# A hand-written order of steps in an attention and two mixture layers, written anew, instruction by instruction on TensorE

## The chip, the cores and the metric

The kernel runs on one core of one Trainium2 chip. The metric is device microseconds (us) of one execution: the median of three runs. One further execution was taken by the hardware profiler; all rows below are from that one. Its engines are called PE (TensorE matmul; PEld is its weight load), DVE (VectorE), ACT (ScalarE), POOL (GpSimd) and SP (SyncE, which here only issues transfers).

## The reference

```python
def reference(q, k, v, ...):               # q, k, v: [4, 8, 576, 64]
    attn = softmax(rot(q) @ rot(k).T / 8) @ v       # 32 heads, rot = rotary embedding
    x = attn as rows [2304, 512]
    x = moe(x, modality_id, ...)    # expert = argmax(x @ w_gate + bias); w * relu(x @ w1[e]) @ w2[e]
    return moe2(x, w_skip, ...)     # rows with x @ w_skip > 0 go through a second such layer, others pass
```

Each mixture layer has 8 experts, w1 of 512x1024 and w2 of 1024x512 each. Every row goes to one expert.

## The kernel before

The heads go through the attention in 16 pairs (p = 0 to 15; of a pair, head a is the odd one, b the even one). The 576 rows of a head are four chunks of 128 and a rest of 64; the rests of both heads share a chunk 4. For precision each operand is split in a high and a low part (`_hi` on ACT, `_lo` on DVE).

The work is cut in named steps. A pair has: `load` (SP), `rope0/1` for q and k (POOL; DVE for p = 0), `qk_tr0/1/2` (PE transposes), `qk_hi`, `qk_lo`, `stackq`, `stackk`, `stack2` (SP transfers, L385, that put parts of q and k beside each other), `v_hi`, `v_lo` (POOL); then for each chunk c and head: `s_mm` (4 matmuls, scores, L413), `s_max` (DVE, L426), `s_exp` (ACT, L430, writes PP), `t_mm` (4 transposes of PP, L508), `t_hi` (ACT, L511), `t_lo` (DVE, L515), `pv` (4 matmuls into O, L542); for chunk 4 `s_mm4`, `s_max4`, `s_exp4`, `t_mm4` (L521), `t_hi4`, `t_lo4` (DVE, L531, two instructions), and `l_mm`, `l_hi`, `l_lo` for the keys of the rest; at last `o_ev` (ACT, L551), `o_mm` (PE, L559), `o_norm` (DVE) and `x_store` (SP). After each fourth pair a batch of 576 rows is routed (`route1` to `route4p`) and its rows are put on the experts' lists with five indirect transfers, `scat0` to `scat4` (POOL, L783; each waits for the one before to land). After pair 11's batch, `ahead1` counts the rows per expert, `ahead2` starts to load the first expert's w1 (SP) and its first list blocks (POOL, L923), and `ahead3` gathers the first rows (POOL, L927), of the first three batches only. After the last pair, `w_hi/lo`, `w2_hi/lo` split the weights, `x_mm0/1` (L1048) transpose the first rows, `m_mm0..3` multiply them with w1, and the loop over blocks of rows begins.

PSUM holds two buffers T (for `qk_tr`, `t_mm`, `t_mm4`, `o_mm`, `route3`), two buffers S of two banks (for `s_mm`, `s_mm4`, `l_mm`) and one O. A step that takes a T buffer waits until the `_lo` (or `o_norm`) of the step two before it on T has read it; S is freed by `s_exp` or `l_lo`.

Each engine executes its instructions in the order in which they are written. That order is a table by hand: each step has a place `POS[name]`, pair p's steps are shifted by 10 p, and all are sorted by place.

Of the kernel before, what the change touches and what calls it, by code (L numbers as in the profile page):

```python
# [36 lines left out]


POS = dict(
    load=-24.542, rope0=-19.7644, rope1=-17.051, v_hi=-8.9048, v_lo=-8.1692, qk_tr0=-13.6414, qk_tr1=-12.311,  # L40
    qk_tr2=-13.5745, qk_hi0=-12.805, qk_hi1=-11.7868, qk_hi2=-12.5767, qk_lo0=-12.3488, qk_lo1=-11.4628,
    qk_lo2=-12.3321, stackq=-11.0409, stackk=-10.1724, stack2=-8.1426, s_mm0a=-6.6353,
    s_max0a=-6.358, s_exp0a=-6.1451, s_mm1a=-5.4139, s_max1a=-5.0991, s_exp1a=-4.5002, s_mm2a=-6.8226,
    s_max2a=-6.3673, s_exp2a=-6.3262, s_mm3a=-4.5196, s_max3a=-4.2702, s_exp3a=-3.2169, s_mm0b=0.5061, s_max0b=0.7184,
    s_exp0b=1.6424, s_mm1b=1.0912, s_max1b=1.4769, s_exp1b=2.2051, s_mm2b=-0.25, s_max2b=0.2617, s_exp2b=0.6341,
    s_mm3b=-2.98, s_max3b=-2.1652, s_exp3b=-0.0102, s_mm4=-3.5823, s_max4=-3.3036, s_exp4=-0.574, l_mma=2.0668,
    l_hia=2.4944, l_loa=2.889, t_mm0a=1.9202, t_hi0a=2.0731, t_lo0a=2.5799, pv0a=3.236, t_mm1a=0.4116, t_hi1a=0.8456,
    t_lo1a=1.3123, pv1a=5.4593, t_mm2a=-1.3533, t_hi2a=-0.4966, t_lo2a=-0.0415, pv2a=3.5848, t_mm3a=-0.2061,
    t_hi3a=0.2252, t_lo3a=0.5436, pv3a=4.2623, pv4a=6.1582, o_eva=7.9328, o_mma=11.0069, o_norma=11.4159,
    l_mmb=2.3316, l_hib=2.7629, l_lob=2.8995, t_mm0b=2.7857, t_hi0b=2.9519, t_lo0b=3.5072, pv0b=8.1446, t_mm1b=7.7762,  # L50
    t_hi1b=9.0218, t_lo1b=9.371, pv1b=9.8111, t_mm2b=4.1992, t_hi2b=5.0136, t_lo2b=5.3907, pv2b=9.1878, t_mm3b=5.9504,
    t_hi3b=5.9975, t_lo3b=6.2737, pv3b=9.6255, pv4b=10.7088, o_evb=11.2681, o_mmb=12.0371, o_normb=12.7355,
    t_mm4=2.9167, t_hi4=2.9782, t_lo4=4.275, r_inv=9.6079, x_store=37.2032, route1=14.3588, route2=22.2105, route2a=21.7, route2b=21.71, route2c=24.2, route2d=24.21, route2e=23.6,
    route2p=25.1759, route3=27.67, route4=27.675, route4p=31.787, scat0=36.7927, scat1=38.8708, scat2=41.493,
    scat3=47.44, scat4=50.0962, ahead1=35.9285, ahead2=50.2465, ahead3=67.8964, load2=10.4862, w_hi0=32.9026,
    w_lo0=41.1441, w_hi1=21.9224, w_lo1=51.4559, w_hi2=47.019, w_lo2=58.0083, w_hi3=69.8951, w_lo3=83.5081,
    x_mm0=28.1772, x_hi0=32.8113, x_lo0=40.2138, x_mm1=44.3621, x_hi1=44.6491, x_lo1=48.9724, m_mm0=54.5051,
    m_hi0=59.1976, m_lo0=60.9832, m_mm1=64.3611, m_hi1=70.0127, m_lo1=86.842, m_mm2=89.4447, m_hi2=98.112,
    m_lo2=121.9228, m_mm3=123.548, m_hi3=141.0569, m_lo3=171.334, route1z=50.3744, route2z=56.2551, route2pz=64.2831,
    route3z=76.7452, route4z=84.8667, route4pz=87.6679, scat0z=91.2443, scat1z=103.827, scat2z=116.579,  # L60
    scat3z=130.8944, scat4z=164.6592, w2_hi0=82.0097, w2_lo0=132.8461, w2_hi1=33.5145, w2_lo1=59.2958, w2_hi2=61.893,
    w2_lo2=91.8739, w2_hi3=15.1559, w2_lo3=69.1493, w2_hi4=109.0836, w2_lo4=179.4963, w2_hi5=91.8978, w2_lo5=142.0314,
    w2_hi6=71.166, w2_lo6=107.7054, w2_hi7=80.8631, w2_lo7=146.4834, const1=-14.5415, const6=-4.5415, const2=-2.2104,
    const3=3.6425, const4=7.7896, const5=-6.3575, warm1=-12.3105, warm2=-6.6348, warm3=-6.8221, warm4=44.3626,
    switch=10.7093,
)


# [1434 lines left out]
```

## Time and profile before

| what | us |
|---|---|
| median of three runs | 791.44 (791.17 to 794.57) |
| the profiled execution | 795.92 |
| its span, first to last instruction | 794.3 |

The profiled execution is 4.48 us above the median; 1.6 us of it lie outside the span. PE is busy in 729.6 us of the span, DVE in 510.8, ACT in 434.8, POOL in 370.2. A busy time is a union of pipelined instructions: four scores that follow each other in 0.52 us are each shown with some 0.3 us.

### The profile page before, as it was taken

To read this page: it belongs to the slowest core of one execution; us is meant where nothing else is said; L and a number is where in the kernel's file an instruction comes from. 1 tells how busy PE (TensorE), PEld (TensorE's weight loads), DVE (VectorE), ACT (ScalarE), POOL (GpSimd) and SP (SyncE) were. 2 spreads that over 40 slices of the span, in tenths; PEclk is the share of its full clock that TensorE was granted. 3 is DMA by queue.
4 is the path that set the end of the run, shared out by engine and by line. 5 is a ranking of instruction groups with operands and counts; after the bars stand their busy time and mean duration, and the time that the engine had idled before them with its cause. 6 is when DMAs were issued, how large, how long until landed. Compare 5 with 4: busy or idle time off the path is not lost. (4 is left out here: it accounts for less than half of the span.)

```text
span 794.3 us, 15318 instructions
## 1 busy us (share of the span) xinstructions
PE 729.6 (92%) x4948; PEld 655.1 (82%) x4948; DVE 510.8 (64%) x1216; ACT 434.8 (55%) x940; POOL 370.2 (47%) x498
## 2 busy tenths in 40 slices
PE   7789999999999999985979999999999979999994
PEld 6688888888888889885878899889988968877773
DVE  5688888888888888873442323232535653588882
ACT  2677777777787787762312222222224542278781
POOL 6385556776676665205343233323434422134532
PEclk9899999999999999996989999999999989999998
DMA  5644445555454553482011111011395401578910
GB/s 136 156 102 117 108 123 129 129 121 124 115 131 121 129 126 80 91 241 69 1 41 35 48 41 54 16 53 41 95 322 173 170 18 38 208 254 293 327 54 18
DMA packets 75197, 92.27 MB, mean 116 GB/s; under 512 B 29440, under 2 KB 50176, under 8 KB 75090
## 3 DMA queue, kind: packets, MB, share of 16 engines
q1 hardware_dynamic: 65938, 73.74, 33.1%
q0 software_dynamic: 7200, 12.46, 5.1%
q10 hardware_dynamic: 1952, 4.85, 2.0%
q8 instruction: 42, 0.69, 0.4%
q14 instruction: 65, 0.53, 0.3%
HBM read 62.11 MB, written 12.95 MB: 95 GB/s over the span
## 5 line engine op out<-in xcount | busy, mean ns | idle before, releaser
L413 PE MATMUL S<-w1s 128*128 128x288 f32 x640 | 116.0, 308 | 3.7 <-ACT PP L430 2.8
L1118 PE MATMUL psY<-w2s,hT 128*128 128x512 f32 x480 | 119.3, 397 | 0.0
L1069 PE MATMUL psM<-xT,w1s 128*128 128x256 f32 x864 | 113.1, 288 | 0.0
L430 ACT ACTIVATE PP<-S,nm 128x576 f32<-128x576 f32 x128 | 95.3, 745 | 30.6 <-DVE nm L426 29.6
L1069 PEld LDWEIGHTS psM<-xT,w1s 128*128 128x128 f32 x864 | 107.4, 192 | 0.6 <-issue 0.6
L426 DVE TENSOR_REDUCE nm<-S 128x1 f32<-128x576 f32 x128 | 96.3, 753 | 8.4 <-PE S L413 7.8
L1118 PEld LDWEIGHTS psY<-w2s,hT 128*128 128x128 f32 x480 | 87.2, 188 | 16.8
L413 PEld LDWEIGHTS S<-w1s 128*128 128x128 f32 x640 | 91.7, 190 | 8.9 <-ACT PP L430 3.6
L515 DVE TENSOR_TENSOR tl<-T,th 128x512 fp32r<-128x512 f32 x128 | 88.0, 688 | 15.9 <-ACT th L511 14.9
L508 PE MATMUL T<-ident,PP 128*128 128x128 f32 x512 | 79.6, 279 | 7.0 <-DVE w1s L382 6.1
L511 ACT CAST th<-T 128x512 fp32r<-128x512 f32 x128 | 74.8, 584 | 19.1 <-PE T L508 18.3
L508 PEld LDWEIGHTS T<-ident,PP 128*128 128x128 f32 x512 | 61.1, 142 | 12.1 <-DVE w1s L382 9.3
L1082 DVE SCALAR_TENSOR_TENSOR hT<-psM,hT 128x512 fp32r<-128x512 f32 x36 | 24.9, 691 | 69.4 <-ACT hT L1077 57.5
L1342 PE MATMUL psM<-w1s,xT 128*128 128x512 f32 x240 | 63.5, 410 | 4.9 <-DVEq L1265 4.5
L1382 PE MATMUL psY<-w2s,hT 128*128 128x512 f32 x240 | 63.8, 403 | 4.4 <-DVE hT L1361 4.4
L1077 ACT ACTIVATE hT<-psM 128x512 fp32r<-128x512 f32 x36 | 21.5, 598 | 76.8 <-PE psM L1069 76.3
L313 POOL TENSOR_TENSOR mem_w<-qkn,mem_w 128x640 f32<-128x640 f32 x30 | 46.5, 1551 | 36.2 <-PE T L350 28.7
L937 POOL DMA_INDIRECT list<-tg,si x20 | 21.1, 1056 | 90.4 <-issue 57.3
L542 PE MATMUL O<-th,vh 128*128 128x288 f32 x256 | 60.2, 316 | 0.5 <-ACT os L551 0.5
L1342 PEld LDWEIGHTS psM<-w1s,xT 128*128 128x128 f32 x240 | 45.0, 193 | 16.3 <-ACTq L1265 4.6
L1382 PEld LDWEIGHTS psY<-w2s,hT 128*128 128x128 f32 x240 | 43.0, 188 | 15.4 <-DVE hT L1361 6.9
L542 PE MATMUL O<-tl,vh 128*128 128x288 f32 x256 | 54.6, 295 | 0.0
(263 smaller groups left out, 1407.2 us busy)
## 6 DMA issues: line engine op xcount, KB each, us to landing
raw<-in_moe_w_dram SPq DMA_DIRECT2D x20, 512.0 KB, 6.4
mem_w<-in_moe_w_dram SPq DMA_DIRECT2D x20, 512.0 KB, 5.7
w1s<-w1s SPq DMA_DIRECT2D x30, 256.0 KB
raw1b<-in_moe_w_dram SPq DMA_DIRECT2D x12, 512.0 KB, 5.8
raw2b<-in_moe_w_dram SPq DMA_DIRECT2D x12, 512.0 KB, 5.8
w1s<-w1s SPq DMA_DIRECT2D x16, 288.0 KB, 3.1
qkn<-in_q_dram SPq DMA_DIRECT2D x16, 256.0 KB, 3.5
qkn<-in_k_dram SPq DMA_DIRECT2D x16, 256.0 KB, 3.5
```

The source lines that it names most:

```text
L313: eng.tensor_tensor(r, x, tb[:, i, 0].unsqueeze(1).broadcast_to([128, 2, 5, D]), op=ALU.mult)
L413: nc.tensor.matmul(ps[:, hf, 0:288], s["wide"][:, o : o + 128], s["K"][h % 2][:, kk, hf * 288 : hf * 288 + 288], start=first and kk == 0, ...
L426: nc.vector.tensor_reduce(st[h // 2]["nm"][:, h % 2, c : c + 1], hs[h]["ps", c][:, :, 0:288], axis=AX.XY, op=ALU.max, negate=True)
L430: nc.scalar.activation(PP[:, c, h % 2 * S : h % 2 * S + S].rearrange("p (a b) -> p a b", a=2), hs[h]["ps", c][:, :, 0:288], AF.Exp, bias=s ...
L508: nc.tensor.transpose(ps[:, c * 128 : c * 128 + 128], PP[:, c, o : o + 128], ident)
L511: nc.scalar.copy(hs[h]["th"][:, j, 0:512], hs[h]["tp", j])
L515: nc.vector.tensor_tensor(s["tl"][:, j, 0:512], s["tp", j], s["th"][:, j, 0:512].bitcast(F32), op=ALU.subtract)
L542: nc.tensor.matmul(s["ot"][:, hf, 0:288], st[h // 2]["vh"][:, h % 2, j].rearrange("p s d -> p (s d)"), w[:, hf * 288 : hf * 288 + 288], st ...
L1069: self.nc.tensor.matmul(ps[:, a], self.w1s[:, wi, dc, fs], x[:, xi, dc], start=(dc == 0 and wi + xi == 0), stop=(dc == 3 and wi == 1))
L1118: nc.tensor.matmul(ps, h[:, hi, f, t * 128 : t * 128 + 128], w2s[:, wi, f], start=(f == 0 and hi + wi == 0), stop=(f == 7 and hi == 1))
L1342: nc.tensor.matmul(ms[hf], x[:, xi, dc], w1s[:, wi, dc, hf * 512 : hf * 512 + 512], start=(dc == 0 and wi + xi == 0), stop=(dc == 3 and xi ...
L1382: nc.tensor.matmul(y, hT[:, hi, f], w2s[:, wi, f], start=(f == 0 and hi + wi == 0), stop=(f == 7 and hi == 1))
```

## The change

Every number of `POS` is another one. A step of PE has now one place for each of its instructions, so that instructions of several steps can alternate. `x_mm` keeps its PSUM buffer by place, so that `x_mm1` may stand before `x_hi0`. No instruction is added or taken away.

For a middle pair p, from one `s_mm2a` to the next (steps of other pairs with their distance; `.0` to `.3` are instructions of a step):

- PE before: s_mm2a, pv0a-1, s_mm0a, pv2a-1, t_mm2b-1, pv3a-1, s_mm1a, pv1a-1, s_mm3a, t_mm3b-1, pv4a-1, qk_tr0+1, s_mm4, qk_tr2+1, s_mm3b, qk_tr1+1, t_mm1b-1, pv0b-1, t_mm2a, pv2b-1, pv3b-1, s_mm2b, t_mm3a, pv1b-1, t_mm1a, s_mm0b, pv4b-1, o_mma-1, s_mm1b, t_mm0a, o_mmb-1, l_mma, l_mmb, t_mm0b, t_mm4.
- PE after: s_mm2a, pv0a.2, pv2a.0, s_mm0a, pv0a.3, rest of pv2a, pv3a.0, t_mm2b, rest of pv3a, pv1a.0, s_mm1a, rest of pv1a, t_mm3b, qk_tr0.0-2, s_mm3a, qk_tr0.3, pv4a, qk_tr2, s_mm4, qk_tr1, t_mm1b, pv0b, half of pv2b, s_mm3b, t_mm2a, rest of pv2b, half of t_mm3a, s_mm2b, rest of t_mm3a, pv3b, pv1b.0, t_mm1a and s_mm0b in turns, pv1b, pv4b and o_mma in turns, s_mm1b, t_mm0a, o_mmb, l_mma, pv0a.0 (of p), l_mmb, t_mm0b, t_mm4, pv0a.1.
- ACT: `v_hi` of p stands ahead of `s_exp2a` (before: `v_hi` of p+1 behind `t_hi1a`), `t_hi2b` ahead of `s_exp0a`, `t_hi3b` ahead of `s_exp1a`; `qk_hi0`, `qk_hi2` and `o_eva` ahead of `s_exp3a`.
- DVE: `t_lo2b` stands ahead of `s_max1a`, `t_lo3b` ahead of `s_max3a`, `qk_lo0` and `qk_lo2` ahead of `s_max4`, `qk_lo1` and `t_lo1b` ahead of `s_max3b`.
- POOL: rope1+1, v_lo, rope0+2 (before: rope0+2, v_lo+1, rope1+2). `scat0` to `scat4` of a batch stand 20 to 26 earlier in the table's scale, of which 15 is the shift that the scores have too.
- SP: x_store-2, load+2, stackq+1, stackk+1, stack2+1 (before: load+2, x_store-4, then the same).
- Start: 68 of the 76 dummy transposes stand ahead of the first `qk_tr0` (before: 36), and `const5` (14 small DVE instructions) ahead of the first `rope0` (before: behind `s_max0a` of pair 0).
- End: `scat0` and `scat1` of pair 11's batch now stand before `s_mm2a` of pair 15, `scat4` between that pair's `s_mm3b` and `s_mm2b`, and the gather `ahead3` before its `s_mm1b`, where it was directly before `x_mm0`; `load2` (w2) follows `x_store` of pair 14. PE goes x_mm0, x_mm1, m_mm3, m_mm0, route3, m_mm1, m_mm2; DVE has six `w2_lo` between `x_lo1` and `m_lo3`, and then route2, route4, `w_lo2`.

```diff
-    load=-24.542, rope0=-19.7644, rope1=-17.051, v_hi=-8.9048, v_lo=-8.1692, qk_tr0=-13.6414, qk_tr1=-12.311,
...
-    s_max0a=-6.358, s_exp0a=-6.1451, s_mm1a=-5.4139, s_max1a=-5.0991, s_exp1a=-4.5002, s_mm2a=-6.8226,
...
+    load=-36.7017, rope0=-33.9451, rope1=-30.111, v_hi=-21.4821, v_lo=-18.1897,
+    qk_tr0=(-30.6061, -30.6042, -30.5936, -30.1223), qk_tr1=(-28.4904, -28.4904, -28.4848, -28.4848),
...
+    s_mm2a=(-22.2316, -22.2316, -22.2316, -22.2316), s_max2a=-21.7162, s_exp2a=-21.4126,
...
+    route2p=7.9451, route3=10.8285, route4=11.1643, route4p=13.5564, scat0=15.9086, scat1=17.0957, scat2=21.6619,
+    scat3=22.8497, scat4=24.3127, ahead1=20.7865, ahead2=24.8061, ahead3=26.173, load2=-9.6073, w_hi0=-4.399,
...
                 for hf in range(2):
-                    nc.tensor.matmul(
+                    yield nc.tensor.matmul(
                         ps[:, hf, 0:288],
...
         def s_mm(h, c):
             ps = hs.setdefault(h, {})["ps", c] = pp.tile([128, 2, 512], F32, name="S")
-            scores(ps, h, c * 128 + (S + 128) * (h % 2), True, True)
+            yield from scores(ps, h, c * 128 + (S + 128) * (h % 2), True, True)
...
         def at(base, name, f, *args):
-            steps.append((base + POS[name], len(steps), f, args))
+            where = POS[name]
+            if isinstance(where, tuple):
+
+                f, args = next, (f(*args), None)
+            else:
+                where = (where,)
+            for x in where:
+                steps.append((base + x, len(steps), f, args))
...
-        ps = self.x_ps = self.bank("T")
+        ps = self.bank("T")
+        self.x_ps = {**self.__dict__.get("x_ps", {}), o: ps}
```

## Rows read from the trace of the kernel before

**Rows 1.** Busy time by stretch: us, then PE, PEld, DVE, ACT, POOL (instructions), PEclk, DMA, GB/s

```profile
39.90:327.80 287.90, 271.33 (x2134) 253.47 (x2133) 246.82 (x490) 229.96 (x550) 186.26 (x227) 1.00 0.49 119
183.53:203.96 20.43, 19.34 (x155) 18.08 (x154) 17.50 (x35) 16.38 (x40) 12.97 (x12) 1.00 0.54 131
```

**Rows 2.** Timeline of PE, `t_mm4`: start us, us, of pair 0 and of pair 14

```profile
39.25 0.60 PE L521 MATMUL T<-ident,PP 128*128 128x128 f32 x4
...
327.18 0.60 PE L521 MATMUL T<-ident,PP 128*128 128x128 f32 x4
```

**Rows 3.** Timeline of PE in one pair; in brackets idle time and what ended it

```profile
208.25 0.43 PE L542 MATMUL O<-th,vh 128*128 128x288 f32 x2
...
208.78 0.68 PE L413 MATMUL S<-w1s 128*128 128x288 f32 x4
209.30 0.60 PE L508 MATMUL T<-ident,PP 128*128 128x128 f32 x4
209.66 0.51 PE L542 MATMUL O<-Y,vh 128*128 128x288 f32 x2
210.27 0.63 PE L347 MATMUL T<-ident,mem_w 128*128 128x128 f32 x4
...
212.15 0.79 PE L413 MATMUL S<-w1s 128*128 128x288 f32 x4
213.50 0.63 PE L347 MATMUL T<-ident,mem_w 128*128 128x128 f32 x4 [0.55 <-DVE w1s L382]
...
214.67 0.42 PE L542 MATMUL O<-tl,vh 128*128 128x288 f32 x2
215.53 0.66 PE L508 MATMUL T<-ident,PP 128*128 128x128 f32 x4 [0.43 <-DVE w1s L382]
```

**Rows 4.** Groups of instructions, whole span: count, busy us, mean ns, idle before

```profile
L430 ACT ACTIVATE PP<-S,nm 128x576 f32<-128x576 f32 x128 | 95.3, 745 | 30.6 <-DVE nm L426 29.6
...
L426 DVE TENSOR_REDUCE nm<-S 128x1 f32<-128x576 f32 x128 | 96.3, 753 | 8.4 <-PE S L413 7.8
...
L515 DVE TENSOR_TENSOR tl<-T,th 128x512 fp32r<-128x512 f32 x128 | 88.0, 688 | 15.9 <-ACT th L511 14.9
...
L511 ACT CAST th<-T 128x512 fp32r<-128x512 f32 x128 | 74.8, 584 | 19.1 <-PE T L508 18.3
```

**Rows 5.** Timeline of the other engines in the pair of Rows 3

```profile
207.22 1.39 DVE L531 TENSOR_TENSOR Y<-T,Y 64x512 fp32r<-64x512 f32 x2
...
211.55 1.04 ACT L370 CAST w1s<-T 128x512 fp32r<-128x512 f32 x3
...
212.50 9.45 SPq L385 DMA_DIRECT2D w1s<-w1s  x10
212.67 0.94 DVE L382 TENSOR_TENSOR w1s<-T,w1s 128x512 fp32r<-128x512 f32 x3
```

**Rows 6.** Dummy transposes (L583) by stretch: us, PE (x), PEld (x), PEclk, DMA, GB/s

```profile
1.70:7.50 5.80, 5.80 (x27) 5.80 (x28) 1.00 0.93 285
7.60:8.70 1.10, 1.08 (x10) 0.84 (x8) 1.00 0.77 193
...
14.40:17.70 3.30, 3.21 (x16) 3.30 (x17) 0.50 0.22 45
```

**Rows 7.** Timeline of the start: first instruction of `const5`, `s_mm4` of pair 0

```profile
21.54 0.43 DVE L193 CAST w<-w8i 128x8 f32<-128x8 int32 x1
...
26.26 1.33 PE L413 MATMUL S<-w1s 128*128 128x288 f32 x8 [2.49 <-ACT PP L430]
```

**Rows 8.** Timeline of the end of the attention and the first block

```profile
329.66 0.98 POOL L783 DMA_INDIRECT list<-g_tg,g_si  x1 [3.24 <-DMA list<-g_tg,g_si]
...
357.55 0.79 POOL L923 DMA_DIRECT2D list<-list  x1 [9.24 <-DMA list<-g_tg,g_si]
...
366.19 1.09 PE L1048 MATMUL T<-ident,xg 128*128 128x128 f32 x4 [10.10 <-DMA xg<-out_dram,tok]
...
402.10 0.17 PE L1168 MATMUL psG<-oh,U 128*128 128x8 bf16 x1 [4.64 <-DVE oh L1165]
```

More of the change, by code (lines that the diff above doesn't have):

```diff
@@ L39 @@
 POS = dict(
-    load=-24.542, rope0=-19.7644, rope1=-17.051, v_hi=-8.9048, v_lo=-8.1692, qk_tr0=-13.6414, qk_tr1=-12.311,
-    qk_tr2=-13.5745, qk_hi0=-12.805, qk_hi1=-11.7868, qk_hi2=-12.5767, qk_lo0=-12.3488, qk_lo1=-11.4628,
-    qk_lo2=-12.3321, stackq=-11.0409, stackk=-10.1724, stack2=-8.1426, s_mm0a=-6.6353,
-    s_max0a=-6.358, s_exp0a=-6.1451, s_mm1a=-5.4139, s_max1a=-5.0991, s_exp1a=-4.5002, s_mm2a=-6.8226,
-    s_max2a=-6.3673, s_exp2a=-6.3262, s_mm3a=-4.5196, s_max3a=-4.2702, s_exp3a=-3.2169, s_mm0b=0.5061, s_max0b=0.7184,
@@ L45 @@
[L45 to L63, printed above, removed]
@@ L64 @@
-    const3=3.6425, const4=7.7896, const5=-6.3575, warm1=-12.3105, warm2=-6.6348, warm3=-6.8221, warm4=44.3626,
-    switch=10.7093,
+    load=-36.7017, rope0=-33.9451, rope1=-30.111, v_hi=-21.4821, v_lo=-18.1897,
+    qk_tr0=(-30.6061, -30.6042, -30.5936, -30.1223), qk_tr1=(-28.4904, -28.4904, -28.4848, -28.4848),
+    qk_tr2=(-29.2463, -29.2463), qk_hi0=-29.4052, qk_hi1=-27.2491, qk_hi2=-29.202, qk_lo0=-29.1934, qk_lo1=-26.9027,
+    qk_lo2=-28.9941, stackq=-25.8754, stackk=-23.011, stack2=-22.5711,
@@ new lines @@
+    s_mm0a=(-22.0577, -22.0577, -22.0577, -22.0577), s_max0a=-21.4825, s_exp0a=-20.8972,
+    s_mm1a=(-21.3076, -21.3076, -21.3076, -21.3076), s_max1a=-20.1346, s_exp1a=-19.5976,
+    s_mm2a=(-22.2316, -22.2316, -22.2316, -22.2316), s_max2a=-21.7162, s_exp2a=-21.4126,
+    s_mm3a=(-20.5225, -20.5225, -20.5225, -20.5225), s_max3a=-19.2489, s_exp3a=-17.295,
+    s_mm0b=(-14.3536, -14.1043, -14.0042, -13.9921), s_max0b=-12.9587, s_exp0b=-12.9046,
+    s_mm1b=(-13.0069, -12.9105, -12.9105, -12.9105), s_max1b=-12.8704, s_exp1b=-12.8563,
@@ new lines @@
+    s_mm2b=(-15.4526, -15.4526, -15.4386, -15.4386), s_max2b=-14.6158, s_exp2b=-14.0784,
+    s_mm3b=(-16.5055, -16.5055, -16.5055, -16.5055), s_max3b=-15.336, s_exp3b=-15.2119,
+    s_mm4=(-19.1859, -19.1807, -19.1807, -19.1807, -19.1807, -19.1807, -19.1807, -19.1331), s_max4=-17.2632,
+    s_exp4=-16.1016, l_mma=(-12.7178, -12.6968, -12.6968, -12.6968, -12.6968), l_hia=-12.6823, l_loa=-12.3966,
+    t_mm0a=(-12.9092, -12.9092, -12.9092, -12.9092), t_hi0a=-12.8887, t_lo0a=-12.6464,
+    pv0a=(-12.6813, -12.3155, -12.1921, -12.051), t_mm1a=(-14.662, -14.3587, -14.3361, -14.0627), t_hi1a=-14.0257,
@@ new lines @@
+    t_lo1a=-12.9105, pv1a=(-11.482, -10.94, -10.9025, -10.9025), t_mm2a=(-16.3817, -16.3207, -16.3207, -16.3207),
+    t_hi2a=-15.4958, t_lo2a=-15.2606, pv2a=(-12.0718, -11.7295, -11.7295, -11.7295),
+    t_mm3a=(-16.0635, -15.4829, -15.3061, -15.3061), t_hi3a=-14.423, t_lo3a=-14.3448,
+    pv3a=(-11.6779, -11.4985, -11.4827, -11.4827), pv4a=(-10.0997, -9.6192), o_eva=-8.4242,
+    o_mma=(-3.8821, -3.1843, -3.04, -3.0069, -3.0069), o_norma=-2.9092,
+    l_mmb=(-12.5752, -12.5752, -12.5752, -12.5752, -12.5752), l_hib=-12.3276, l_lob=-12.2073,
@@ new lines @@
+    t_mm0b=(-12.4134, -12.3969, -12.3818, -12.3818), t_hi0b=-12.2316, t_lo0b=-11.9973,
+    pv0b=(-6.7017, -6.7017, -6.7017, -6.5129), t_mm1b=(-7.8953, -7.8953, -7.8953, -7.4024), t_hi1b=-6.7199,
+    t_lo1b=-6.1978, pv1b=(-5.2632, -4.5696, -3.9061, -3.5847), t_mm2b=(-11.6405, -11.6405, -11.6405, -11.6405),
+    t_hi2b=-11.3076, t_lo2b=-11.3076, pv2b=(-6.5077, -6.5077, -6.2903, -6.172),
+    t_mm3b=(-10.8705, -10.8705, -10.8705, -10.8705), t_hi3b=-9.8594, t_lo3b=-9.5279,
+    pv3b=(-5.2659, -5.2659, -5.2659, -5.2659), pv4b=(-3.1789, -3.0274), o_evb=-3.008,
@@ new lines @@
+    o_mmb=(-2.908, -2.9041, -2.9041, -2.8421, -2.8421), o_normb=-2.5794,
+    t_mm4=(-12.3715, -12.3715, -12.3715, -12.3715), t_hi4=-11.4863, t_lo4=-11.4473, r_inv=-4.0473, x_store=-1.9435,
+    route1=-0.138, route2=22.2105, route2a=0.0711, route2b=2.3991, route2c=5.809, route2d=6.9931, route2e=3.0369,
+    route2p=7.9451, route3=10.8285, route4=11.1643, route4p=13.5564, scat0=15.9086, scat1=17.0957, scat2=21.6619,
+    scat3=22.8497, scat4=24.3127, ahead1=20.7865, ahead2=24.8061, ahead3=26.173, load2=-9.6073, w_hi0=-4.399,
@@ new lines @@
+    w_lo0=-2.8576, w_hi1=-10.8843, w_lo1=-10.3037, w_hi2=-3.048, w_lo2=429.3001, w_hi3=-3.3916, w_lo3=-3.1985,
+    x_mm0=-2.5275, x_hi0=-2.4128, x_lo0=-2.2031, x_mm1=-2.35, x_hi1=-2.1246, x_lo1=-2.0387, m_mm0=48.2393,
+    m_hi0=181.3328, m_lo0=1552.441, m_mm1=611.0564, m_hi1=1628.6892, m_lo1=1629.4085, m_mm2=1553.3863, m_hi2=1625.391,
+    m_lo2=1629.4891, m_mm3=6.3202, m_hi3=25.9681, m_lo3=44.977, route1z=0.3768, route2z=49.5846, route2pz=83.0433,
+    route3z=164.2886, route4z=197.8744, route4pz=247.5439, scat0z=1554.3317, scat1z=1556.1501, scat2z=1556.8609,
@@ L66 @@
+    scat3z=1626.076, scat4z=1629.4488, w2_hi0=3.7676, w2_lo0=6.9592, w2_hi1=0.3352, w2_lo1=2.9321, w2_hi2=-0.7596,
+    w2_lo2=-0.5096, w2_hi3=-2.8008, w2_lo3=-0.4501, w2_hi4=4.8596, w2_lo4=46.894, w2_hi5=-2.8731, w2_lo5=-2.4756,
+    w2_hi6=5.4516, w2_lo6=35.4726, w2_hi7=-0.1195, w2_lo7=1.6545, const1=-11.4827, const6=-0.4859, const2=-2.0544,
+    const3=21.5765, const4=22.9241, const5=-41.9989, warm1=-42.8466, warm2=-28.4242, warm3=-36.7926, warm4=1629.4689,
+    switch=-2.9023,
 )
@@ L441, in s_mm4 @@
             for i in range(2):
-                scores(ps, 2 * p + i, 512 + 64 * i, i == 0, i == 1)
+                yield from scores(ps, 2 * p + i, 512 + 64 * i, i == 0, i == 1)
         def s_max4(p):
@@ L507, in t_mm @@
             for c in range(4):
-                nc.tensor.transpose(ps[:, c * 128 : c * 128 + 128], PP[:, c, o : o + 128], ident)
+                yield nc.tensor.transpose(ps[:, c * 128 : c * 128 + 128], PP[:, c, o : o + 128], ident)
         def t_hi(h, j):
```

24 lines of the change are left out of this document (12 added, 12 removed).

## The prediction

> **What bounds the kernel now.** I read four views. The busy time by stretch comes first [rows 1]: from 39.9 to 327.8 us PE is busy in 94% of the time, DVE in 86% and ACT in 80%. No engine is full, yet none has much room. The timeline of one step that occurs once in each pair [rows 2] gives the pace: from `t_mm4` of pair 0 to that of pair 14 it is (327.18 - 39.25) / 14 = 20.57 us for a pair. The timeline of PE inside a pair [rows 3] shows where PE's 20.4 us go. Scores, transposes and `pv` that follow each other without a wait start every 0.52, 0.36 and 0.53 us for four instructions (208.78 to 209.30, 209.30 to 209.66, 208.25 to 208.78). At three places the next start comes later than that: `qk_tr0` (210.27 - 209.66 - 0.26 = 0.35), `qk_tr1` (213.50 - 212.15 - 0.53 = 0.82) and `t_mm2a` (215.53 - 214.67 - 0.26 = 0.60), 1.77 us together. The last two name DVE L382, that is `qk_lo`: PE waits for a T buffer. The busy column hides this, since ends of matmuls overlap with waits. At last the end of the attention [rows 8]: PE has nothing from 356.1 (366.19 - 10.10) to 366.19, because the first rows come late, and they come late because the list block waited 9.24 us for a scatter to land.
>
> DVE can't be read as free: in the 20.43 us of the one pair shown it works 17.50 [rows 1]. A pair can't fall below that, whatever PE's order.
>
> **Instructions.** None is added. PE has 155 multiplications and 154 weight loads in a pair [rows 1], so each instruction loads its own weights already, and taking turns between steps costs no further load. I price the splitting at nothing; the bounds are the 0.08 us by which `pv` starts later than the pace at some changes of step, and as much gained.
>
> **The middle pairs.** I walked once around the new order with the old durations: a reduction 0.75 us, an exponential 0.74, a `t_hi` 0.58, a `t_lo` 0.69 [rows 4], `t_lo4` 1.39, three `qk_hi` 1.04, three `qk_lo` 0.94 [rows 5], and 0.1 us from a reader's end to the next writer of the buffer. Clock zero is the first `l_mma`.
>
> - `qk_tr1` takes the buffer of `qk_tr0`. Before, ACT did `s_exp3a` and DVE `s_max4` ahead of its readers. Now `qk_hi0` and `qk_lo0` come first; the buffer is free at 9.66, when PE has just ended `s_mm4` at 9.53. Wait 0.13 instead of 0.82.
> - `t_mm2a` takes that of `qk_tr1`. `qk_lo1` now precedes `s_max3b`, and PE has `t_mm1b`, `pv0b`, two `pv2b` and `s_mm3b` to do first (1.7 us of work where it had 0.9). Free at 11.82, PE there at 11.74. Wait 0.08 instead of 0.60.
> - `qk_tr0` takes that of `t_mm2b`, whose `t_lo2b` still stands behind the 1.39 us of `t_lo4`: free at 6.88, and PE is there at 6.53. Wait 0.35, as before. Behind it now stands `s_mm3a`, so `s_max3a` starts later too; DVE covers this with `s_max1a` and `t_lo3b` (until 8.07, and the scores are ready at 7.9).
> - `t_mm3b` now stands ahead of `s_mm3a` and waits for `t_lo4` itself: free at 6.18, PE there at 5.90. New wait 0.28.
> - `s_mm3b` needs the S buffer of `s_exp3a`, which ACT now does after `qk_hi` and `o_eva`: free at 10.57, PE comes at 11.21. Nothing.
> - The `pv0a.0` and `.1` fill time in which PE waited for `t_mm4` and `s_mm2a`: 0.25 gained.
>
> The balance is 0.69 + 0.52 + 0.25 - 0.28 = 1.18, plus some small waits that I don't count apart; I take 19.2 us for a pair. 14 pairs of 20.57 - 19.2 give **19.2 us**. Bounds: by the walk without any delay between engines 18.7 (26 us), and half of the balance (8 us).
>
> What else is queued: SP issues ten transfers for `stack` in 9.45 us from `qk_hi2` on [rows 5]. In the walk this begins at 9.2, and the first scores of the next pair come at 20.8, so 2 us remain. `load` waits on SP for `v_lo`, which now comes later (6.4 of the walk); the three transfers behind it end at 8.4, before the `stack` ones are due. POOL does its 12.97 us [rows 1] with one pair more of lead; a batch's `route1` between `rope0` and `rope1` can push `v_lo` and so SP by some 2 us, once in four pairs. It is covered by those 2 us; without cover it would cost 3 x 2 = 6 us. `x_store` two pairs earlier is three issues ahead of `load`; nothing reads the rows so soon.
>
> **The start.** 68 dummies now precede `qk_tr0`. Before, 27 took 5.80 us and the next 10 took 1.08 [rows 6], 0.215 and 0.108 us each. The PEclk column reads 1.00 in both stretches, but where it reads 0.50 the pace is 0.2 again, so the slow pace is that of the level of 1.2 GHz. The 68 take 5.8 + 41 x 0.108 = 10.2 us and end at 11.9, when `qk_tr0` once could begin after 36 (8.7). The Trainium skill, page "TensorE: Matmul & The Clock Gate", section "Part 4: PE-mode transpose", says that transposes don't make the full clock engage; rows 6 speak against it, since only transposes ran before the pace doubled. `const5` (14 instructions from 21.54 on; 3 us by my estimate, more than the wait that it caused) goes ahead of `rope0` on DVE, partly into its wait for the first load. Together I let the first scores start 1.5 us later, since `qk_tr2` needs the second `rope` anyway. Back come the 2.49 us that PE waited at 26.26 for the exponential behind `const5` [rows 7], and by my estimate 1 us of latencies after it. Net **-2 us**; bounds +3.4 (all dummies in the way, nothing back) and -5.
>
> **The end.** The idle 10.1 us go if the rows land when PE ends. From `t_mm4` of pair 14 PE needed 356.1 - 327.18 = 28.9 us to the end of the attention, now some 27.5. A scatter takes POOL 3.24 + 0.98 = 4.2 us with its wait for the one before [rows 8]. By its new place `scat0` is issued some 7 us ahead of that `t_mm4`, so `scat4` 17 us later, at +10. It lands 3.2 us after (as the others) or 9.2 (as this one did, with the weights' loads on the queues; w2 now waits for pair 14's `x_store`). From the list's load to `x_mm0` it took 366.19 - 357.55 = 8.6. So the rows land at +22 to +28 against PE's 27.5. I keep 1 us of wait. After that the pace is POOL's: in the row of 402.10 PE waits for a selection that hangs on POOL's work, 35.9 us after `x_mm0`. `route2` now stands on DVE behind six `w2_lo`; one us later. Net **-8 us**; bounds 0 (the gather is as late as before) and -12 (all the idle time and the 1.4 us that PE ends earlier).
>
> **Sum.** 795.92 - 19.2 - 2 - 8 = 766.7 for the profiled execution; the median is 4.48 lower: 762.2. I say **762**, its own range 749 to 772.
>
> **Rivals.**
>
> 1. The stall only moves. PE's order of steps is nearly the old one, DVE works 17.5 us in it, and a wait that is shorter for `qk_tr1` comes back at the next T buffer. For it: 0.28 at `t_mm3b` is such a return. Against it: four changes on DVE and ACT all put readers of T first. Only start and end and half a us per pair remain: 791.4 - 10 - 3 = 778 to 784. Chance 0.20.
> 2. A convoy at the T buffers, the slower side. `t_mm3b` and `qk_tr0` now stand on PE ahead of `s_mm3a`. PE is in order: if `t_lo4` slips (its `t_hi4` has `t_hi0b` ahead on ACT, and `v_hi` behind it delays `s_exp2a`), `s_mm3a` slips with it, DVE runs out of reductions, and the next `t_lo` is late again. One more reduction (0.75) waited for at each of `t_mm3b`, `qk_tr0` and `qk_tr2`, and 0.5 for `s_mm1a`, give 19.2 + 2.75 = 21.95 a pair, 14 x 1.38 = +19, less 10: 800. It decides from 21.3 a pair on (0.7 above today's, which uses up the 10). Chance 0.12.
> 3. The end gives nothing: scatters still behind w1's load, or w2, now loaded later, holds up ACT's `w2_hi5` in front of `x_hi0`. 770. Chance 0.10.
> 4. The dummies never reach the quick pace. 68 x 0.215 = 14.6 us, `qk_tr0` at 16.3 instead of 11.9: 766. Rows 6 speak against it; chance 0.02. This is what the Trainium skill's sentence above ("TensorE: Matmul & The Clock Gate", Part 4) would make of it.
> 5. All of it cancels, a pair at some 21.2: 788 to 795. Chance 0.06.
>
> The forecast has 0.50. From 748 (26 + 5 + 12 us gained) to 785 lie the forecast and rivals 1, 3 and 4, 0.82. Faster by over 0.5% (4 us, about what a measurement of this kernel can tell from no change): 0.82; within it 0.06; slower 0.12.
>
> **What would show it.** `t_mm4` of pairs 0 and 14 in the new profile some 269 us apart; no wait over 0.2 us before `qk_tr1` and `t_mm2a`, one of 0.3 before `t_mm3b`; `x_mm0` with an idle time of 0 to 2 us; the first dummies ending near 12 us. Wrong is the forecast if the pair stays above 20 us, where I would look at what DVE does while PE waits for T; or if PE idles before `x_mm0` as long as now.

## The result, and the profile after

The changed kernel takes 768.97 us (median of 4 runs, 767.88 to 772.4) where the kernel before takes 793.01 beside it (4 runs, 791.17 to 797.8): 0.9695 of it, 95% interval 0.9639 to 0.9752. The forecast was 762 in a range of 748 to 785; it was right in sign and range, and 7 us too low. The profiled execution took 767.88 us, its span is 766.2.

The walk through it goes by the same views as before. First `t_mm4` on PE's timeline, of pairs 0, 1, 2 and 14:

```profile
34.34 0.60 PE L538 MATMUL T<-ident,PP 128*128 128x128 f32 x4
...
53.47 0.60 PE L538 MATMUL T<-ident,PP 128*128 128x128 f32 x4
...
79.16 0.60 PE L538 MATMUL T<-ident,PP 128*128 128x128 f32 x4
...
309.16 0.60 PE L538 MATMUL T<-ident,PP 128*128 128x128 f32 x4
```

From pair 2 to 14 a pair takes (309.16 - 79.16) / 12 = 19.17 us; before it was 20.57 over all 14 [rows 2], and 20.52 over these twelve. But the one pair from 53.47 to 79.16 takes 25.69. The busy time by stretch (columns as in [rows 1]) tells the two apart:

```profile
53.47:79.16 25.69, 21.91 (x154) 20.77 (x153) 17.44 (x35) 16.59 (x41) 15.65 (x13) 0.87 0.48 114
79.16:309.16 230.00, 229.96 (x1832) 218.51 (x1831) 207.35 (x423) 197.20 (x473) 157.00 (x202) 1.00 0.54 130
174.92:194.02 19.10, 19.10 (x154) 18.18 (x153) 17.16 (x35) 16.40 (x41) 11.86 (x12) 1.00 0.58 140
```

From pair 2 on PE is busy for 229.96 of 230.00 us, with the same instructions: no idle time of PE is left in this column, though it can hide a late start. In one middle pair, the timeline of PE where before waited 0.55 and 0.43 us [rows 3] has no brackets at `qk_tr1` (182.89) and `t_mm2a` (185.08):

```profile
179.22 0.69 DVE L532 TENSOR_TENSOR tl<-T,th 128x512 fp32r<-128x512 f32 x1
179.47 0.60 PE L525 MATMUL T<-ident,PP 128*128 128x128 f32 x4
180.06 0.52 PE L364 MATMUL T<-ident,mem_w 128*128 128x128 f32 x3
...
181.46 0.34 PE L367 MATMUL T<-ident,mem_w 64*128 64x64 f32 x2
181.73 1.32 PE L430 MATMUL S<-w1s 128*128 128x288 f32 x8
182.89 0.60 PE L364 MATMUL T<-ident,mem_w 128*128 128x128 f32 x4
183.32 0.60 PE L525 MATMUL T<-ident,PP 128*128 128x128 f32 x4
...
184.55 0.69 PE L430 MATMUL S<-w1s 128*128 128x288 f32 x4
185.08 0.60 PE L525 MATMUL T<-ident,PP 128*128 128x128 f32 x4
```

What changed sides is to be seen in it: `s_mm4` (181.73, eight instructions) now stands between `qk_tr2` and `qk_tr1`, and `s_mm3b` (184.55) between `pv` and `t_mm2a`. PE works while ACT and DVE empty the T buffer. Counted by starts, as the forecast counted, `qk_tr1` now comes 0.12 us late (182.89 - 181.73 - 8 x 0.13), `t_mm2a` on time (185.08 - 184.55 - 0.53) and `qk_tr0` still 0.23 late (180.06 - 179.47 - 0.36): it starts 0.15 us after `t_lo2b` (DVE, 179.22) has read its buffer. The three were 1.77 us and are 0.35: the 1.42 between them is what a pair gained (1.35 to 1.40), to the error of such a count. The groups of the page say the same from the other side: ACT's exponentials and DVE's reductions, which idled 30.6 and 8.4 us [rows 4], now idle 8.0 and 3.4.

```profile
L447 ACT ACTIVATE PP<-S,nm 128x576 f32<-128x576 f32 x128 | 95.8, 748 | 8.0 <-DVE nm L443 7.5
L443 DVE TENSOR_REDUCE nm<-S 128x1 f32<-128x576 f32 x128 | 94.7, 750 | 3.4 <-PE S L430 3.4
```

The end of the attention, answering [rows 8] (POOL's list load, PE's `x_mm0`, PE's first block selection):

```profile
326.49 0.79 POOL L947 DMA_DIRECT2D list<-list  x1 [6.27 <-DMA list<-g_tg,g_si]
...
339.25 0.63 PE L1073 MATMUL T<-ident,xg 128*128 128x128 f32 x4 [0.31 <-DMA xg<-out_dram,tok]
341.32 0.63 PE L1073 MATMUL T<-ident,xg 128*128 128x128 f32 x4 [1.45 <-DMA xg<-out_dram,tok]
...
376.25 0.17 PE L1193 MATMUL psG<-oh,U 128*128 128x8 bf16 x1 [2.30 <-DVE oh L1190]
```

The wait of 10.10 us is 0.31 and 1.45. The profiled 795.92 - 767.88 = 28.0 us divide so: `t_mm4` of pair 0 comes 39.25 - 34.34 = 4.9 earlier; the 14 pairs take 274.8 in place of 287.9, 13.1 less (19.6 from 14 x (20.57 - 19.17), less 6.5 in the one long pair); from `t_mm4` of pair 14 to `x_mm0` 30.1 in place of 39.0, 8.9 less; from there to the selection 37.0 in place of 35.9, 1.1 more; behind it 2.2 less.

The long pair has its own row. On POOL, in and around it:

```profile
44.56 1.57 POOL L336 TENSOR_TENSOR mem_w<-mem_w 128x640 f32<-128x640 f32 x1
51.94 0.29 POOL L240 PARTITION_BROADCAST mbb<-mbr  x1 [5.81 <-issue]
52.10 0.29 POOL L242 CAST mf<-mi 128x20 f32<-128x20 int32 x1
59.23 1.54 POOL L330 TENSOR_TENSOR mem_w<-qkn,mem_w 128x640 f32<-128x640 f32 x1 [6.84 <-PE T L525]
```

And on PE, `qk_tr2`, which needs that rope (L330 to L336):

```profile
64.07 0.37 PE L367 MATMUL T<-ident,mem_w 64*128 64x64 f32 x1 [3.78 <-POOL mem_w L336]
```

Between two ropes POOL stands still for 5.81 us before `const2`'s broadcast and 6.84 behind it: 13.1 us (46.13 to 59.23) for 0.45 us of work. The releaser named for the 6.84, a `t_mm` on PE, shares no tile with the rope, so something else held POOL. The records of POOL's sequencer, which the timeline leaves out, have an instruction MODIFY_POOL_CONFIG at 46.08 and 46.11, with the line of the broadcast, and again at 52.32 and 52.36, with the line of the next rope: a change of GpSimd's program and, it seems, the change back. PE's wait is only 3.78 of the 6.5 us that the pair loses. During it the granted clock falls to 0.50 and stays there from 62.96 to 69.78 (0.87 over the pair); at that level `s_mm4` of this pair takes 2.29 us (64.36), where it takes 1.32 at 181.73. What holds POOL is tested below. The Trainium skill, page "GPSIMD Engine Reference", section "2.1 Instruction dispatch", says that the first call of a freshly loaded GpSimd program costs some 6 us that no instruction of the profile shows; the 5.81 agree with that.

### The profile page after: what moved, and what is told of

Read it like the earlier page. It is cut to its first block, busy times and chain, and to the rows that moved or that the text cites. A ratio compares the mean times of both kernels' runs of the same rounds, so it can differ in the third digit from the quotient of the medians.

```text
span 766.2 us, 15348 instructions
## 1 busy us (share of the span) xinstructions
PE 725.8 (95%) x4948; PEld 654.8 (85%) x4948; DVE 504.0 (66%) x1216; ACT 435.3 (57%) x940; POOL 359.4 (47%) x498
## 3 DMA queue, kind: packets, MB, share of 16 engines
q10 hardware_dynamic: 1952, 4.85, 2.1%
## 5 line engine op out<-in xcount | busy, mean ns | idle before, releaser
L430 PE MATMUL S<-w1s 128*128 128x288 f32 x640 | 124.8, 321 | 3.0 <-DVE w1s L398 1.2
L430 PEld LDWEIGHTS S<-w1s 128*128 128x128 f32 x640 | 95.9, 195 | 6.7 <-ACT PP L447 1.6
L443 DVE TENSOR_REDUCE nm<-S 128x1 f32<-128x576 f32 x128 | 94.7, 750 | 3.4 <-PE S L430 3.4
L525 PE MATMUL T<-ident,PP 128*128 128x128 f32 x512 | 87.4, 275 | 1.1 <-DVE w1s L399 0.4
L559 PE MATMUL O<-th,vh 128*128 128x288 f32 x256 | 74.0, 329 | 0.6 <-ACT os L568 0.5
L525 PEld LDWEIGHTS T<-ident,PP 128*128 128x128 f32 x512 | 63.1, 141 | 3.6 <-DVE tl L532 0.8
L1102 ACT ACTIVATE hT<-psM 128x512 fp32r<-128x512 f32 x36 | 21.5, 598 | 74.1 <-PE psM L1094 73.6
L559 PE MATMUL O<-tl,vh 128*128 128x288 f32 x256 | 61.7, 306 | 0.0
L330 POOL TENSOR_TENSOR mem_w<-qkn,mem_w 128x640 f32<-128x640 f32 x30 | 47.0, 1568 | 19.1 <-PE T L367 11.9
```

The lines of the kernel that those rows point to most:

```text
L330: eng.tensor_tensor(r, x, tb[:, i, 0].unsqueeze(1).broadcast_to([128, 2, 5, D]), op=ALU.mult)
L430: yield nc.tensor.matmul(ps[:, hf, 0:288], s["wide"][:, o : o + 128], s["K"][h % 2][:, kk, hf * 288 : hf * 288 + 288], start=first and kk ...
L525: yield nc.tensor.transpose(ps[:, c * 128 : c * 128 + 128], PP[:, c, o : o + 128], ident)
L559: yield nc.tensor.matmul(s["ot"][:, hf, 0:288], st[h // 2]["vh"][:, h % 2, j].rearrange("p s d -> p (s d)"), w[:, hf * 288 : hf * 288 + 28 ...
```

## Experiments

Ratios are to the kernel before, run beside each; the kernel after has 0.9695, and 0.01 is 7.9 us.

**The long pair: the broadcast away, or SP's issues away.** `row_by_dma`:

```
-        self.mbr = self.wp.tile([1, 2, E], F32, name="mbr", bufs=1)
-        nc.sync.dma_start(self.mbr, self.mb.unsqueeze(0))
+        self.mbb = self.wp.tile([128, 2, E], F32, name="mbb", bufs=1)
+        nc.sync.dma_start(self.mbb, self.mb.unsqueeze(0).broadcast_to([128, 2, E]))
...
-        nc.gpsimd.partition_broadcast(self.mbb, self.mbr)
```

> The modality bias row is laid on all 128 partitions by the DMA of constants1 that loads it, in place of GpSimd's partition_broadcast in constants2; nothing else differs from the kernel after. Theory (GpSimd's change of program): in the kernel after, GpSimd stands still for 5.81 us before the broadcast and for 6.84 us behind it, 12.7 us for 0.45 us of work, between the two ropes of a pair, and this makes the pair from the second t_mm4 to the third 25.69 us where the others take 19.2. Without it that pair falls to 19.2 to 19.6, rope1 follows rope0 on GpSimd within 1 us, and the time falls by some 6 us, to 762 to 764 (0.961 to 0.964 of before). Rival (SP's queue: constants6's four issues of 3.1 us stand ahead of the next pair's load): the pair stays above 24 us and the time at 767 to 770.

Measured: 760.3 us (6 runs), 0.9595 [0.9562, 0.9628]. By stretch, the pair that was long, and then POOL between its ropes:

```profile
54.39:73.50 19.11, 19.11 (x154) 18.19 (x153) 17.17 (x35) 16.40 (x41) 11.06 (x9) 1.00 0.63 152
```

```profile
45.84 1.57 POOL L334 TENSOR_TENSOR mem_w<-mem_w 128x640 f32<-128x640 f32 x1
47.34 0.21 POOL L240 CAST mf<-mi 128x20 f32<-128x20 int32 x1
47.50 1.58 POOL L328 TENSOR_TENSOR mem_w<-qkn,mem_w 128x640 f32<-128x640 f32 x1
```

Both gaps go with the broadcast (and so do the four MODIFY_POOL_CONFIG), and the pair falls by 6.6 us. The span is 8.0 shorter; the other 1.4 are not explained by it. This version is faster than both kernels.

`const6_late`: `const6=23.2985` for `-0.4859`.

> constants6 (four issues on SP, 3.1 us) goes from before the fifth pair's load to behind the seventh's; the broadcast stays. Theory (GpSimd's change of program): nothing, the pair from the second t_mm4 to the third stays at 25 to 26 us and the time at 767 to 770 (0.967 to 0.971 of before). Rival (SP's queue): that pair falls below 22.6 us and the time to 763 to 766.

Measured: 768.22 us, 0.969 [0.9657, 0.9722]; the pair takes 26.28. SP's four issues are not the cause.

**The broadcast in other places.** `before_row` is the edit of `row_by_dma` in the kernel before; `const2_early` leaves the broadcast in the kernel after and sets `const2=-10.05`.

> The kernel before with the bias row laid on all partitions by a DMA, without the broadcast on GpSimd. Theory (the price of the broadcast is that of its place: in before it stands where GpSimd is early): the time falls by 0 to 2.5 us only (0.997 to 1.000 of before), against the 8 us that the same edit took from the kernel after. Rival (the broadcast costs its 13 us of GpSimd wherever it stands): 5 us or more, under 0.994.

> The kernel after with constants2 (the broadcast stays) behind rope1 of the third pair, ahead of v_lo of the second, where GpSimd is idle for 3.2 and 2.7 us on both sides. Theory (13 us less the room at that place): the pair from the second t_mm4 to the third falls from 25.7 to 20 to 23 us, the time to 763 to 766 (0.963 to 0.967 of before). Rival (any place on GpSimd costs the same): the pair and the one behind it lose 6 us together, the time stays at 767 to 770.

Measured: `before_row` 1.000 [0.9982, 1.0019], so there the broadcast cost nothing. `const2_early` 768.16 us, 0.9714 [0.9688, 0.9741], the pair 25.79: no gain, my theory fell. POOL and PE show where it went:

```profile
40.26 0.29 POOL L240 PARTITION_BROADCAST mbb<-mbr  x1 [6.12 <-issue]
40.42 0.29 POOL L242 CAST mf<-mi 128x20 f32<-128x20 int32 x1
47.66 1.55 POOL L347 TENSOR_TENSOR vh<-vn,vh 128x640 fp32r<-128x640 f32 x1 [6.95 <-ACT th L528]
```

```profile
59.17 1.30 PE L430 MATMUL S<-w1s 128*128 128x288 f32 x4 [4.52 <-DMA w1s<-w1s]
```

```profile
SPq L316 <- POOL vh L347: 9.3, 1, 9.3
```

Now `v_lo` is late (47.66 for 37.03). SP's next load of v waits 9.3 us for it (the waits of SP's queue: total, times, longest), the ten `stack` transfers stand behind that load on SP, and the scores wait for them. The place was free on POOL, but not on SP behind it. In before the broadcast stands one pair earlier:

```profile
29.77 0.29 POOL L223 PARTITION_BROADCAST mbb<-mbr  x1 [6.17 <-DMA w1s<-w1s]
...
37.56 1.53 POOL L313 TENSOR_TENSOR mem_w<-qkn,mem_w 128x640 f32<-128x640 f32 x1 [7.33 <-issue]
```

The same 6 and 7 us, in the first pair, where `before_row` shows that they cost nothing.

**The middle pairs: whole steps.** `steps_whole` gives every tuple of places its last value, so `t_mm1a=(-14.0627, -14.0627, -14.0627, -14.0627)` and so on.

> Every TensorE step of the attention stands whole again, all of its instructions at the place of its last one; the order of the steps on ACT, DVE, POOL and SP is that of the kernel after. Theory (the stalls went because ACT and DVE take qk_hi, qk_lo and t_lo earlier): no wait of more than 0.3 us before qk_tr1 and t_mm2a comes back, a steady pair takes 19.2 to 19.6 us, the time 769 to 776 (0.970 to 0.979 of before). Rival (the places of single instructions are what covers the waits): waits of 1 us and more a pair come back, a pair takes over 20.2 us, the time 785 or more.

Measured: 773.04 us, 0.9764 [0.9731, 0.9796]: the theory's side, 4.8 us over `const6_late` on the same chip. A plain pair, and one with a batch's routing in it:

```profile
176.35:195.71 19.36, 19.17 (x155) 18.17 (x154) 17.18 (x35) 16.51 (x40) 11.22 (x10) 1.00 0.52 133
215.08:235.49 20.41, 19.31 (x157) 18.33 (x156) 17.45 (x37) 16.49 (x40) 15.28 (x20) 1.00 0.61 141
```

```profile
222.11 0.33 PE L367 MATMUL T<-ident,mem_w 64*128 64x64 f32 x2 [0.17 <-DVE tl L532]
223.37 0.18 PE L779 MATMUL T<-g_oh,U 128*128 128x40 bf16 x1 [0.93 <-DVE w1s L399]
```

In a plain pair the places of single instructions are worth 0.2 us. In the three pairs with routing they are worth 1.1 (20.41 for 19.27): `route3` (L779) waits for `qk_lo` there, and in the kernel after seven of the eight instructions of `s_mm4` stand ahead of it and cover the wait; here the whole `s_mm4` stands behind it, since each step went to the place of its last instruction. A whole `s_mm4` ahead of `route3` wasn't run, so the 1.1 are the price of this place and not shown to be that of whole steps.

**Parts of the new order in the kernel before.** Three kernels with whole steps take over ever more of it.

```
before_three:  s_max4=-2.30  s_max3b=-1.40  s_exp3a=-2.50
before_cover:  s_max4=-2.30  s_max3b=-1.40  s_mm4=-3.57  s_mm3b=-1.5
before_seven:  as before_cover, and s_mm3a=-3.60  s_max3a=-3.50  pv4a=6.41
```

> The kernel before with three numbers changed: s_max4 behind qk_lo2 and s_max3b behind qk_lo1 on DVE, s_exp3a behind qk_hi2 on ACT; TensorE's order is untouched. Theory (the two stalls come from this order alone): the waits before qk_tr1 (0.82 us) and t_mm2a (0.60 us) fall under 0.25 us each, a pair from 20.5 to 19.3 to 19.7 us, the time by 12 to 17 us (0.979 to 0.985 of before). Rival (the stall only moves): the waits come back elsewhere, before a scores step or a pv step, a pair stays above 20.2 us and the time within 4 us of before.

> The kernel before with four numbers changed: on TensorE s_mm4 stands behind qk_tr2 in place of ahead of it, and s_mm3b stands just ahead of t_mm2a in place of ahead of qk_tr1; on DVE s_max4 stands behind qk_lo2 and s_max3b behind qk_lo1, as they must follow. s_exp3a is where before has it. Theory (the two scores steps are moved to where TensorE would have waited, and cover the way over ACT and DVE): the waits before qk_tr1 (0.54 us in a middle pair) and t_mm2a (0.43 us) both fall under 0.2 us, no new one comes, a pair takes 19.4 to 19.8 us for 20.5, the time falls by 10 to 15 us (0.981 to 0.987 of before). Rival (the stall moves again): a wait of 0.5 us or more shows before another step, a pair stays above 20.2 us, the time within 4 us of before or above it.

> The four moved numbers of the run with two moved scores steps, and three more: s_mm3a and pv4a stand between qk_tr0 and qk_tr2 on TensorE, as they do in the kernel after, with s_max3a behind t_lo3b on DVE. All steps are whole. Theory (each wait is covered by the step moved into it, and the 0.62 us that was left before qk_tr2 is covered by these two): no wait over 0.25 us in a middle pair, a pair of 19.2 to 19.5 us where the four numbers gave 19.88, the time another 5 to 9 us lower, 0.979 to 0.984 of before. Rival (with whole steps a wait is always left): the pair stays at 19.8 us or more and the time above 0.987 of before.

Measured: 1.0081 [1.0054, 1.0107], 0.9903 [0.9873, 0.9932] and 1.0162 [1.0134, 1.0189]; a middle pair takes 20.92, 19.88 and 21.36 us. All waits of PE in one pair, of the three in this order:

```profile
199.22 0.79 PE L413 MATMUL S<-w1s 128*128 128x288 f32 x4 [1.15 <-ACT PP L430]
201.85 0.66 PE L508 MATMUL T<-ident,PP 128*128 128x128 f32 x4 [0.45 <-DVE w1s L382]
```

```profile
187.78 0.33 PE L350 MATMUL T<-ident,mem_w 64*128 64x64 f32 x2 [0.62 <-DVE tl L515]
```

```profile
197.41 0.63 PE L347 MATMUL T<-ident,mem_w 128*128 128x128 f32 x4 [0.88 <-DVE tl L515]
201.57 0.63 PE L347 MATMUL T<-ident,mem_w 128*128 128x128 f32 x4 [1.22 <-DVE w1s L382]
```

With DVE's and ACT's order alone (three numbers) the wait before `qk_tr1` goes, `t_mm2a` keeps its 0.45, and `s_mm3b` gets 1.15: its S buffer is freed by `s_exp3a`, which now waits on ACT behind `qk_hi2`. The kernel gets slower: the rival had the place right and the time too low, and the theory fell. With the two scores steps as covers (four numbers) both old waits are gone and 0.62 comes before `qk_tr2`, a result between theory and rival. With `s_mm3a` moved as well (seven) the theory fell again: `s_exp3a`, still ahead of `qk_hi0` on ACT, waits for the later `s_mm3a`, and so `qk_hi0`, `qk_lo0` and `qk_tr1` (1.22) are late in turn; and `qk_tr0`, with `s_mm3a` no longer ahead of it, waits 0.88. This chain is read from the order and the waits. In the kernel after, `s_exp3a` stands behind `qk_hi2` and `s_mm3b` far behind both. No part of the order gave the whole; two made it worse. The last link, `s_exp3a` behind `qk_hi2` on top of the seven, wasn't run.

**The start.** `dummies_back` sets `warm1=-28.43, warm3=-22.1, warm2=-21.4`; `const5_back` sets `const5=-21.48`.

> The kernel after with the start's dummy transposes where before has them: 36 first, 20 behind qk_tr1, 12 behind the first scores step, 8 behind the second. Theory A (the dummies only fill waiting, and each kernel pays one stretch of 5 to 6 us at the lower clock somewhere in its first 35 us): the first scores come within 0.7 us of 18.06, the fifth chunk of scores still waits under 1 us, the time stays within 1.5 us of the kernel after (0.967 to 0.972 of before). Theory B (the dummies' places decide the clock of the first pair): the lower clock comes at 24 to 34 us as in before, the first t_mm4 comes 2 to 4 us later than 34.34, the time is 770 to 773.

> The kernel after with constants5 (2.5 us of small instructions on DVE) behind the first pair's second s_max, where before has it, in place of ahead of the first rope. Theory (its place costs nothing at the start, since the ropes then meet GpSimd's rope of the next pair and go slower, as one of them did in before with 2.23 us for 0.89): the first scores come within 0.8 us of 18.06 and the 2.5 us stand in front of the later s_max, the first t_mm4 comes 0 to 2.5 us later than 34.34, the time is 768 to 771. Rival (the first rope 0.8 to 2.5 us earlier carries through): the first scores and the first t_mm4 come 0.8 to 2.5 us earlier, the time is 765.5 to 767.5.

Measured: 767.68 us, 0.9693 [0.9665, 0.9721], and 768.47 us, 0.9702 [0.9672, 0.9731]. With the dummies back the first `t_mm4` comes at 34.43, 0.1 later. By stretch, the first scores with the dummies back, then those of the kernel after:

```profile
18.98:24.15 5.17, 5.17 (x44) 4.75 (x42) 3.05 (x6) 2.01 (x5) 3.84 (x3) 1.00 0.49 121
```

```profile
18.06:24.16 6.10, 5.29 (x20) 4.45 (x20) 3.45 (x5) 2.79 (x7) 4.64 (x4) 0.50 0.61 152
```

The scores start 0.9 later but at a granted clock of 1.00 (2.4 GHz), where those of the kernel after run at 0.50 (1.2 GHz) to 24.16. The one pays for the other. The lower level is not gone with the dummies back, it stands earlier: 0.50 from 11.3 to 18.1, where PE is busy for 3.7 of the 6.8 us, against 15.2 to 25.4 in the kernel after. So theory A holds in the time, and each of these two kernels has its one stretch; it holds neither in its 0.7 us nor in the size of the stretch (6.8 and 10.2 us for 5 to 6). What makes the scores late stands on DVE and POOL of `dummies_back`:

```profile
10.12 2.23 DVE L334 TENSOR_TENSOR mem_w<-qkn,mem_w 128x320 f32<-128x320 f32 x2
10.47 1.53 POOL L330 TENSOR_TENSOR mem_w<-qkn,mem_w 128x640 f32<-128x640 f32 x1 [2.78 <-PE T L367]
```

These two DVE instructions took 0.89 in the kernel after. POOL's first rope, released by PE's first `qk_tr2`, starts beside them here; 68 dummies ahead of `qk_tr0` hold that rope back to 11.62.

With `const5` back the first `t_mm4` comes at 36.66, 2.3 later: PE waits 1.27 us for an exponential at 25.65, and the clock stays at 0.50 until 29.1. The long pair gives back 0.74 (24.95 for 25.69); the median doesn't show the rest.

**The end.** `end_back` and `end_back2` set `scat0=21.5, scat1=23.6, scat2=26.2, scat3=32.1, scat4=34.8, ahead2=34.9, load2=-4.8, ahead3=37.45`, and `w_hi1`, `w_lo1` behind the load (-4.85, -4.83) and behind `x_hi1` (-2.12, -2.10).

> The kernel after with the scatters of each batch, the loads of the first expert's weights (with the first split behind them) and the first rows' gather as late beside the attention as in before; the x_mm0 steps and all else stay. Theory (what lets x_mm0 follow the attention without waiting is that scatters, list load and gather stand some 12 us earlier): x_mm0 waits 6 to 11 us again, the time rises by 6 to 11 us, to 774 to 780 (0.977 to 0.985 of before). Rival (the end gives nothing, GpSimd's later work sets when TensorE goes on): the wait comes back but the time stays within 2 us of the kernel after.

> The late scatters, weight loads and gather once more, with the first weight split behind the second x_hi on ACT, so that ACT's last o_ev doesn't stand behind a split that waits for its weights. Theory (the rows themselves are late): x_mm0 waits 6 to 11 us and the time is 774 to 778 (0.977 to 0.983 of before). Rival (only the split was late): x_mm0 waits under 3 us and the time is within 2.5 us of the kernel after, 0.966 to 0.973.

Measured: 774.25 us, 0.9776 [0.9747, 0.9806], and 776.04 us, 0.9806 [0.9781, 0.9832]: 6.4 and 8.8 us over the kernel after, as the theory has it, but not at its place. In the first of them, on PE, ACT and POOL:

```profile
344.95 2.41 PE L577 MATMUL T<-IIg,os 128*128 128x72 f32 x10 [6.81 <-ACT os L568]
```

```profile
340.48 3.88 ACT L982 CAST w1s<-raw 128x1024 fp32r<-128x1024 f32 x4 [5.62 <-DMA raw<-in_moe_w_dram]
344.27 0.63 ACT L568 COPY os<-O 128x576 f32<-128x576 f32 x1
```

```profile
339.77 1.11 POOL L951 DMA_INDIRECT xg<-out_dram,tok  x1 [0.69 <-DMA raw<-in_moe_w_dram]
```

PE waits in `o_mm`, since ACT's last `o_ev` stands behind splits that wait for their weights. The gather is issued 8.4 us later than in the kernel after (339.77 for 331.36), hidden under the same wait. Moving one split of four (`end_back2`) left the other three there, and PE waits 10.84 at the same step, though the gather comes only 2.0 us later than in the kernel after:

```profile
348.56 2.41 PE L577 MATMUL T<-IIg,os 128*128 128x72 f32 x10 [10.84 <-ACT os L568]
```

```profile
333.32 1.11 POOL L951 DMA_INDIRECT xg<-out_dram,tok  x1 [0.69 <-POOL tok L1042]
```

So in `end_back2` PE waits for the late weights, through the splits on ACT, and not for the rows, and the theory of that run fell; in `end_back` the rows come late as well, behind the same wait. That the early group of scatters, weights and gather is worth 6 to 9 us is shown; what the rows alone would cost is not.

## Why the forecast was right, and where it was not

- **Middle pairs.** Forecast 19.2 us a pair, measured 19.17; 19.2 us in all, measured 19.6 without the long pair. The waits before `qk_tr1` and `t_mm2a` are gone, as said: 0.12 and 0 by starts, for 0.13 and 0.08 in the walk. Of the two that I kept or added, 0.28 before `t_mm3b` isn't there, and 0.23 of the 0.35 before `qk_tr0` is, behind `t_lo4` and `t_lo2b` as the walk has it. Part of the working leaned to one side: its case against rival 1 rests on ACT and DVE taking the readers of T first, and only for `t_mm2a` does it count PE's own work as cover. The order of ACT and DVE alone makes the kernel slower (`before_three`); PE's own order, with scores steps set where PE would have waited, is the other half (`before_cover`), and ACT's `s_exp3a` must fit both. The balance of 1.18 gives 19.39 a pair; the 0.19 more that I took had no row. With whole steps a plain pair measured 19.36, so those 0.2 came from the places of single instructions, which I had priced at nothing: to that extent 19.2 was luck. `steps_whole` as a whole costs 4.8 us, the larger part in the three pairs with routing.
- **Rivals.** None of the five came. But for rival 1 (the stall only moves) and rival 2 (a convoy at the T buffers) the partial orders show that they were near: 0.62 at `qk_tr2` is the first, and 21.36 us a pair has the size of the second, though its chain runs over ACT's `s_exp3a`.
- **What I left out.** `const1`, `const2` and `const6` also got new places, and I costed none of them; `const2` stood between the ropes of pairs 1 and 2 and stands now between `rope0` and `rope1` of pair 3. POOL's queue past `const2` is the step that failed: the row of the broadcast with its two gaps stood in the profile before, with 13.96 us between the ropes around it (23.60 to 37.56), and my "one pair more of lead" of POOL is just what moved the ropes of a later pair behind it. It costs 6.5 us in the pair and 8 in the time.
- **Start.** Forecast -2, measured -4.9. The 68 dummies took 9.20 us (forecast 10.2, their end at 10.90 for 11.9) and so ran fast, which settles rival 4; the first scores came at 18.06 (two of their instructions at 16.02), not 1.5 us later than the 18.21 of before. `const5` ran from 4.44 to 6.95, for the most part while DVE waited for the first load, so that the first rope came only 0.8 later (6.98 for 6.17). In the second rope the same two instructions took 1.34 less. That is the dummies' doing and not that of `const5`: 2.23 comes back in `dummies_back`, with `const5` early, and in `const5_back` they take 0.89. I had not foreseen it. Before, and after:

```profile
9.31 2.23 DVE L317 TENSOR_TENSOR mem_w<-qkn,mem_w 128x320 f32<-128x320 f32 x2
```

```profile
10.12 0.89 DVE L334 TENSOR_TENSOR mem_w<-qkn,mem_w 128x320 f32<-128x320 f32 x2
```

- **End.** Forecast -8 (9 less before `x_mm0`, 1 more behind), measured -8.9 and +1.1. `scat4` was issued 10.1 us behind `t_mm4` of pair 14 (forecast 10) and the list load then waited 6.27 us more; PE was at `x_mm0` after 29.8 us, not 27.5, and the rows after 30.1, not 22 to 28: from the list's load to `x_mm0` it took 12.8 us (339.25 - 326.49) for the 8.6 that I had read from before. Both were late alike, so that the small wait is luck in part.
- **Sum.** The forecast for the profiled execution was 766.7 and it took 767.88: 6.5 us were lost in the long pair, and against the forecast 0.4 were gained in the other pairs, 2.9 at the start and 2.2 behind the selection; the end came as forecast, to 0.2 us. The last gain, 2.2, has no cause that I know. The median missed by more, 768.97 for 762.2: I took 4.48 us off because the profiled execution of before lay that far above its median, and that of after lies 1.1 below its own. The runs of the kernel after differ by 4.5 us among themselves, so that this close a hit says little.
